# Linear attention into a channel mix on one core: halved crossbar transposes, g kept out of w_k for the first group, w_v loaded in two parts, and a new instruction order

## The chip, the cores and the metric

The kernel runs on one core of one Trainium2 chip. The metric is device time in microseconds (us): the time of one execution. Before the change it is 204.62 us, the median of 4 runs (204.26 to 205.23). The engines are named as in the profile: PE (TensorE, matrix multiply), PEld (its weight loads), DVE (VectorE), ACT (ScalarE), POOL (GpSimd) and SP (SyncE). Matrix operands are bf16 in on-chip memory; inputs and output are fp32 in device memory.

## The reference

Shapes are 8 batches, 8 heads, 576 positions, head width 64; the mix has model width 512 and hidden width 1024.

```python
def _attn_ref(q, k, v, g_norm):
    kv = np.einsum('bhsd,bhse->bhde', k, v)
    out = np.einsum('bhsd,bhde->bhse', q, kv)
    rms = np.sqrt(np.mean(out * out, axis=-1, keepdims=True) + 1e-06)
    return (out / rms * g_norm).astype(np.float32)

def _moe_ref(x, mu_k, mu_r, w_k, w_v, w_r):
    x_prev = np.concatenate([np.zeros((B, 1, D)), x[:, :-1, :]], axis=1)
    xk = mu_k * x + (1.0 - mu_k) * x_prev
    xr = mu_r * x + (1.0 - mu_r) * x_prev
    k = np.maximum(xk @ w_k, 0.0)
    v = k * k @ w_v
    r = 1.0 / (1.0 + np.exp(-(xr @ w_r)))
    return (r * v).astype(np.float32)
```

The attention output, with heads side by side, is the `x` of the second function. `g_norm` scales each head's 64 columns alike, so it may be multiplied into `x`, or into the rows of `w_k` and `w_r`.

## The kernel before

The work has two kinds of stage. Attention runs per batch (576 rows). The mix runs per group of 512 rows, so nine groups, numbered 0 to 8, cover the eight batches. Group 0 lies wholly in batch 0; group 1 needs the last 64 rows of batch 0 and most of batch 1, and so on.

The names below are those of the pieces in the order list; the number after the name is the batch or group, and what follows the point is a pair of heads (0 to 3), two of them for the larger batches, or a part. A `#2` marks the second use of a name; in batch 0 this is mostly the second stretch of columns.

Attention of a batch: `load` brings q, k and v by a GpSimd DMA that also converts to bf16. `kv` multiplies k by v on PE (`kvc` copies it out of PSUM). `qtr` transposes q on PE with `qc` copying it out, for batches 0 to 2. For batches 3 to 7 (`BY_DMA`) `ql` copies q into a buffer `q2` with pairs of heads side by side, `qt` transposes it with a DMA issued by SP, and `gate`, a one-element GpSimd copy that reads the transposed tile, holds the loads of the next batch until the transpose has landed: the loads follow `gate` in GpSimd's order. `u` multiplies q by kv on PE, `uc` copies it out, `sq` squares it, `ss` sums the squares on PE, `rr` is the reciprocal square root on ACT, and `mul` gives x, laid out so that the previous row is reached by an offset of 96 columns. For batches 5 to 7 the root goes through device memory (`ro`, `rb`). Then `d` is x minus the previous row; `mk`/`mr` scale it by mu, and `xk`/`xr` add the previous row.

Batch 0 is done in finer pieces, by one pair of heads for its first 256 rows and by two pairs for the other 320 (`mixed`, line 439), and the first half of group 0's k is summed pair by pair as the pairs arrive (`k0.a`, line 476); `k0.b` (line 763) is the rest.

The mix of a group: `k` (8 blocks of 128 hidden columns), `relu` on ACT, `ksq` on DVE, `r` and `sig` (line 795 and 800), `v` (line 817), `out` on DVE, which multiplies v by the sigmoid, and `store` by SP. The PSUM tiles of k, r and v come from one pool of two (`mm`); the output tiles from a pool of three, and `q2` has one buffer. A group's last step stands at line 834.

`w_k`, `w_r` and `w_v` are loaded by GpSimd. g is multiplied into `w_k` (two halves of hidden columns, `g.w_k0` and `g.w_k1`) and `w_r` in place on DVE, before any use.

All instructions stand in one list, `ORDER`: every piece in turn, with the engine after a colon where there is a choice. The list fixes the order within each engine's queue, SP's and GpSimd's DMA issues among them. `idle:n` puts n small matmuls on zeros into PE's queue. The costs, `land` and `due` values given to `add` were used to find an order and have no effect in the run.

```python
def load_w(dst, s, due, land, name):
    def fn(_):
        nc.gpsimd.dma_start(out=dst, in_=s.rearrange("(c p) n -> p c n", p=128))
...
gate = add({"POOL": 0.3}, lambda _: nc.gpsimd.tensor_copy(out=turned, in_=qT.t[0:1, 0, 0:1]), deps=[c],
```

Of the kernel before, what the change touches and what calls it, by code (L numbers as in the profile page):

```python
# [15 lines left out]
setup ident loadq0.2 loadk0.2 first_k first_q cast_q:DVE cast_k:DVE first_v table cast_v:DVE idle:61 qtr0.0  # L16
qc0.0#2:ACT idle:2 kv0.0 kvc0.0:ACT qtr0.1 qc0.1#2:ACT loadv0.2 idle:6 kv0.1 kvc0.1:ACT ident9 edge qc0.1:DVE
qc0.0:DVE idle:1 u0.0 uc0.0:DVE sq0.0 small tr9 u0.1 u0.0#2 uc0.1:ACT sq0.1 cols loadv0.6 loadk0.6 loadq0.4
uc0.0#2:ACT sq0.0#2 idle:5 ss0.0 rr0.0 mul0.0 idle:3 ss0.1 rr0.1 mul0.1 d0.0 mr0.0:DVE idle:1 ss0.0#2 rr0.0#2
mul0.0#2 kv0.3 kvc0.3:DVE d0.1 qtr0.2 qc0.2#2:ACT d0.0#2 mk0.0:DVE xk0.0 loadq0.6 qtr0.3 qc0.3#2:ACT qc0.3:ACT  # L20
loadv0.4 qc0.2:ACT loadk0.4 idle:7 kv0.2 idle:4 u0.3 uc0.3:DVE sq0.3 kvc0.2:ACT u0.2#2 uc0.2#2:ACT u0.2 uc0.2:ACT
sq0.2 idle:13 ss0.3 w_k0 g.w_k0 sq0.2#2 ss0.2 rr0.2 mul0.2 rr0.3 idle:8 ss0.2#2 rr0.2#2 d0.2 mul0.3 loadq1.0 k0.a0.0
idle:6 qtr1.0 mk0.0#2:ACT qc1.0:ACT mk0.2:DVE mul0.2#2 mr0.1#2:DVE loadk1.0 mk0.1#2:ACT mk0.1:DVE xr0.0 xk0.2
idle:14 k0.a0.2 loadv1.0 kv1.0 d0.2#2 xk0.1 k0.a0.1 mk0.2#2:DVE kvc1.0:ACT mr0.0#2:ACT u1.00 d0.3 mk0.3#2:DVE
mk0.3:DVE xk0.3 xk0.2#2 xk0.0#2 xr0.0#2 w_k1 uc1.00:ACT sq1.00 u1.01 uc1.01:ACT sq1.01 g.w_k1 mr0.2:DVE mr0.2#2:DVE
k0.a0.3 relu0.00 mr0.3:ACT k0.b0 ss1.00 k0.a1.0 relu0.10 mr0.1:DVE ksq0.10 xr0.2 ss1.01 rr1.01 rr1.00 k0.a1.3
k0.a1.1 k0.a1.2 relu0.01 mr0.3#2:ACT loadq1.4 w_r k0.b1 xr0.1 ksq0.00 xr0.3 loadv1.4 qtr1.2 loadk1.4 kv1.2 g.w_r:DVE
xr0.2#2 r0.2 relu0.11 qc1.2:DVE kvc1.2:DVE u1.10 uc1.10:ACT r0.3 sig0.1 u1.11 r0.0 r0.1 sig0.0 ksq0.11 ksq0.01
sq1.10 uc1.11:DVE sq1.11 ss1.11 ss1.10 rr1.10 mul1.0 d1.0 xk1.0 xr1.0 w_v v0.2.0 v0.2.1 v0.3.0 rr1.11 mul1.2 d1.2
xk1.2 v0.3.1 out0.1 v0.0.0 v0.0.1 v0.1.0 loadk2.0 loadq2.0 qtr2.2 qtr2.0 v0.1.1 qc2.0:DVE out0.0 qc2.2:ACT k1.0  # L30
loadv2.0 kv2.0 kvc2.0:ACT k1.1 relu1.0 xr1.2 loadq3.0 ql3.3:DVE ql3.0:DVE ql3.1:DVE ql3.2:ACT loadk3.0 loadv3.0
u2.10 uc2.10:DVE sq2.10 u2.01 uc2.01:ACT sq2.01 k1.2 k1.3 k1.4 u2.00 u2.11 store0.0#2 qt3 store0.0 store0.1#2
relu1.1 uc2.11:DVE uc2.00:ACT sq2.00 ksq1.1 sq2.11 ksq1.0 k1.5 ss2.01 rr2.01 relu1.2 k1.6 ss2.10 rr2.10 store0.1
gate3 loadq4.0 k1.7 relu1.3 ss2.00 rr2.00 mul2.0 r1.0 r1.1 sig1.0 r1.2 r1.3 ss2.11 sig1.1 loadv4.0 kv3.0 ksq1.2
ksq1.3 v1.0.0 v1.0.1 v1.1.0 v1.1.1 d2.0 xk2.0 rr2.11 kvc3.0:ACT u3.11 uc3.11:ACT u3.10 uc3.10:ACT v1.2.0 v1.2.1
u3.01 u3.00 uc3.01:ACT v1.3.0 v1.3.1 mul2.2 d2.2 out1.0 xk2.2 ql4.1:ACT uc3.00:ACT ql4.3:DVE loadk4.0 store1.0#2
store1.0 ql4.2:DVE ql4.0:DVE qt4 gate4 loadq5.0 out1.1 store1.1 k2.4 k2.5 relu2.2 sq3.00 sq3.10 xr2.2 sq3.01 sq3.11
ksq2.2 xr2.0 k2.6 k2.7 relu2.3 ksq2.3 k2.2 ss3.10 rr3.10 k2.3 relu2.1 ss3.11 rr3.11 mul3.2 ss3.00 k2.0 rr3.00 d3.2
k2.1 relu2.0 ss3.01 r2.0 rr3.01 mul3.0 ksq2.0 r2.1 sig2.0 kv4.0 r2.2 r2.3 kvc4.0:DVE ksq2.1 u4.10 u4.01 sig2.1
uc4.01:ACT uc4.10:ACT v2.0.0 v2.0.1 v2.1.0 xk3.2 d3.0 sq4.01 xk3.0 sq4.10 u4.11 uc4.11:ACT u4.00 ql5.2:DVE  # L40
uc4.00:ACT ql5.1:ACT sq4.11 ql5.3:DVE ql5.0:DVE loadk5.0 loadv5.0 v2.2.0 v2.2.1 v2.1.1 out2.0 ss4.10 rr4.10 v2.3.0
xr3.0 ss4.01 v2.3.1 out2.1 k3.4 k3.5 ss4.11 rr4.01 relu3.2 xr3.2 ksq3.2 k3.0 rr4.11 mul4.2 sq4.00 d4.2 xk4.2 k3.1
relu3.0 ksq3.0 qt5 store1.1#2 store2.1#2 k3.6 k3.7 kv5.0 kvc5.0:ACT relu3.3 k3.2 u5.10 uc5.10:DVE u5.11 uc5.11:ACT
ksq3.3 sq5.11 gate5 loadq6.0 k3.3 relu3.1 ksq3.1 u5.00 uc5.00:ACT sq5.00 u5.01 uc5.01:ACT r3.0 sq5.01 sq5.10 r3.1
sig3.0 ss4.00 ql6.3:ACT ql6.1:DVE ql6.2:DVE ql6.0:DVE store2.0#2 store2.0 store2.1 v3.0.0 v3.0.1 v3.1.0 v3.1.1
out3.0 rr4.00 mul4.0 d4.0 xk4.0 r3.2 ss5 r3.3 v3.2.0 v3.2.1 v3.3.0 v3.3.1 rr5 xr4.2 sig3.1 out3.1 xr4.0 loadv6.0
loadk6.0 kv6.0 k4.6 k4.7 relu4.3 k4.2 k4.3 kvc6.0:DVE qt6 u6.11 uc6.11:ACT ro5 relu4.1 store3.0 store3.0#2 u6.00
uc6.00:DVE sq6.00 k4.0 u6.01 uc6.01:ACT u6.10 uc6.10:DVE ksq4.3 k4.1 relu4.0 k4.4 k4.5 relu4.2 r4.0 r4.1 sig4.0
ksq4.1 ksq4.0 sq6.10 sq6.11 sq6.01 ss6 rr6 ro6 rb5 mul5.0 d5.0 gate6 loadq7.0 r4.2 ksq4.2 ql7.0:DVE ql7.3:DVE
ql7.2:DVE ql7.1:DVE xk5.0 mul5.2 r4.3 sig4.1 v4.2.0 v4.2.1 v4.3.0 v4.3.1 d5.2 xk5.2 out4.1 v4.0.0 v4.0.1 v4.1.0  # L50
v4.1.1 loadk7.0 loadv7.0 kv7.0 out4.0 xr5.2 k5.4 k5.5 relu5.2 k5.6 k5.7 kvc7.0:DVE xr5.0 qt7 u7.10 u7.01 uc7.10:DVE
# [51 lines left out]
def kernel(  # L103
# [97 lines left out]
    def dve_us(n, rate=1):  # L201
        return (0.13 if rate == 4 else 0.07) + n / rate / 960
# [696 lines left out]
```

## Time and profile before

| what | value |
|---|---|
| median of 4 runs | 204.62 us |
| the profiled execution: whole, and its span | 205.23 us, 203.4 us |
| PE busy | 194.3 us, 96% of the span, 1645 matmuls |
| DVE busy | 147.6 us, 73% |
| ACT busy | 113.6 us, 56% |
| POOL busy | 33.4 us, 16% |
| filler matmuls (line 713) | 131 |
| granted PE clock | full |
| mean DMA rate over the span | 156 GB/s |

The span is the time between the first and the last instruction of the profiled execution; the rest of its 205.23 us lies around it. Busy time of PE counts filler matmuls as well, and matmuls overlap, so it is no measure of useful work by itself. In the chain of waits each row is a start, a length and what the end of the kernel depended on there. In the timeline a row is a run of like instructions, with the engine's idle time before it and what ended it in brackets. In a table by windows each column after the stretch and its width is the busy time and count of one engine, then the granted clock, the DMA share and GB/s. A DMA row gives the number of issues, the KB of each and the microseconds from issue to landing.

### The profile page before, as it was taken

What the parts mean: (1) busy time and instruction counts of PE and PEld (TensorE: products, weight loads), DVE (VectorE), ACT (ScalarE), POOL (GpSimd) and SP (SyncE); (2) the same over time, 40 slices, a digit from 0 to 9 for tenths busy, and PEclk for the clock granted to TensorE, in tenths of its full rate; (3) what the DMA queues carried; (4) which work ended last, traced back from release to release, by engine and by line L of the source; (5) the groups of instructions that cost most, each with busy time, mean ns of one, the idle gap of its engine ahead of it and who ended that gap; (6) DMA issues with size and microseconds to landing.
All of it is one profiled execution on the core that took longest, in us unless ns stands there. A gap on an engine that the chain in (4) does not pass through costs nothing.

```text
span 203.4 us, 4096 instructions
## 1 busy us (share of the span) xinstructions
PE 194.3 (96%) x1645; PEld 102.6 (50%) x1645; DVE 147.6 (73%) x324; ACT 113.6 (56%) x145; POOL 33.4 (16%) x52
## 2 busy tenths in 40 slices
PE   7879699999999999999999999999999999999991
PEld 7757484454553454444447744444444444444451
DVE  1588968998589889799688799899658984232341
ACT  2276867827895598756992683286473226622500
POOL 6965404000050013005005202000200000000000
PEclk9999999999999999999999999999999999999999
DMA  6999999999989989998999999840180116000643
GB/s 177 195 202 205 204 205 206 204 203 219 197 174 182 226 162 124 202 206 188 215 199 221 180 196 159 232 140 3 52 220 3 42 37 205 29 0 0 179 131 108
DMA packets 39800, 31.69 MB, mean 156 GB/s; under 512 B 13636, under 2 KB 34916, under 8 KB 39780
## 3 DMA queue, kind: packets, MB, share of 16 engines
q0 software_dynamic: 21488, 18.11, 57.4%
q1 hardware_dynamic: 17620, 12.42, 25.8%
q10 hardware_dynamic: 672, 0.89, 1.3%
q8 instruction: 13, 0.21, 0.4%
q14 instruction: 7, 0.06, 0.1%
HBM read 35.33 MB, written 9.46 MB: 220 GB/s over the span
## 4 chain that ended last, share of the span: by engine, by line
PE 82%; DMA 8%; POOL 3%; ACT 2%; DVE 1%; issue 1%; SPq 0%; DVEq 0%
PE mm L743 26%; PE mm L817 24%; PE mm L795 15%; DMA qT<-q 5%; DMA k<-in_k_dram 4%; PE at L599 3%; PE at L520 3%; PE at L651 2%; PE mm L763 2%; PE at L834 2%; PE mm L834 2%; PE mm L476 2%; PE at L577 1%; ACT uT L184 1%; POOL q L273 1%
## 5 line engine op out<-in xcount | busy, mean ns | idle before, releaser
L743 PE MATMUL mm<-xk,w_k 128*128 128x512 bf16 (+1 forms) x288 | 59.0, 356 | 0.0
L817 PE MATMUL mm<-w_v,sqk 128*128 128x512 bf16 x256 | 58.3, 379 | 0.0
L747 ACT ACTIVATE relu<-mm 128x1024 bf16<-128x1024 f32 x36 | 37.0, 1027 | 36.2 <-PE mm L743 31.8
L743 PEld LDWEIGHTS <-w_k 128*128 128x128 bf16 x288 | 27.2, 98 | 26.1 <-issue 1.6
L817 PEld LDWEIGHTS <-sqk 128*128 128x128 bf16 x256 | 24.5, 98 | 29.1 <-issue 0.9
L795 PE MATMUL mm<-w_r,xr 128*128 128x512 bf16 x144 | 34.1, 380 | 0.0
L750 DVE TENSOR_TENSOR sqk<-relu 128x1024 bf16<-128x1024 bf16 x32 | 21.4, 686 | 12.0 <-ACT relu L747 11.8
L821 DVE TENSOR_TENSOR out<-mm,sig 128x1024 f32<-128x1024 f32 x16 | 19.5, 1221 | 12.8 <-PE mm L817 12.1
L800 ACT ACTIVATE sig<-mm 128x1024 bf16<-128x1024 f32 x18 | 18.3, 1024 | 16.7 <-PE mm L795 16.5
L795 PEld LDWEIGHTS <-xr 128*128 128x128 bf16 x144 | 13.4, 98 | 15.8 <-issue 0.9
L193 ACT ACT_TABLE_LOAD x14 | 18.0, 1283 | 1.4 <-PEq L883 1.2
L693 DVE TENSOR_SCALAR md<-d,cols 128x576 bf16<-128x576 bf16 x56 | 18.5, 371 | 0.3
L184 ACT CAST uT<-at 128x576 bf16<-128x576 f32 x21 | 12.8, 642 | 7.2 <-PE at L599 7.0
L667 DVE TENSOR_TENSOR xT<-uT,rs 128x1152 bf16<-128x1152 bf16 x14 | 10.5, 753 | 4.6 <-ACT rs L655 4.6
L713 PE MATMUL mm<-zero 128*128 128x128 bf16 x131 | 11.8, 253 | 1.1 <-DVE zero L243 1.1
L606 DVE TENSOR_TENSOR sq<-uT 128x576 bf16<-128x576 bf16 x28 | 11.9, 452 | 0.6 <-ACT uT L184 0.3
L655 ACT ACTIVATE rs<-at,eps 128x576 bf16<-128x576 f32 x16 | 11.6, 742 | 0.9 <-PE at L651 0.7
L634 POOL DMA_DIRECT2D rs<-rd x6 | 3.8, 642 | 45.6 <-DVE md L693 20.8
L713 PEld LDWEIGHTS <-zero 128*128 128x128 bf16 x131 | 10.0, 116 | 2.4 <-DVE zero L243 1.1
L696 DVE TENSOR_TENSOR xr<-md,xT 128x1152 bf16<-128x1152 bf16 x14 | 10.6, 759 | 0.5
L696 DVE TENSOR_TENSOR xk<-md,xT 128x1152 bf16<-128x1152 bf16 x14 | 10.6, 759 | 0.5
L679 DVE TENSOR_TENSOR d<-xT 128x1152 bf16<-128x1152 bf16 x14 | 10.6, 754 | 0.3
(81 smaller groups left out, 168.6 us busy)
## 6 DMA issues: line engine op xcount, KB each, us to landing
out_dram<-out SPq DMA_DIRECT2D x22, 192.0 KB, 2.5
k<-in_k_dram POOLq DMA_DIRECT2D x6, 576.0 KB, 13.4
q<-in_q_dram POOLq DMA_DIRECT2D x6, 576.0 KB, 8.5
v<-in_v_dram POOLq DMA_DIRECT2D x6, 576.0 KB, 12.0
out_dram<-out SPq DMA_DIRECT2D x23, 128.0 KB, 5.9
rs<-rd POOLq DMA_DIRECT2D x6, 288.0 KB, 5.7
out_dram<-out SPq DMA_DIRECT2D x22, 64.0 KB, 2.4
w_k<-in_moe_w_k_dram POOLq DMA_DIRECT2D x2, 512.0 KB, 10.6
```

The source lines that it names most:

```text
L184: nc.scalar.copy(out=dst, in_=src)
L193: nc.scalar.preload_act_table_set(name)
L693: nc.vector.tensor_scalar(out=get(md)[:, hp], in0=d.t[:, hp], scalar1=cols[:, m0 + hp:m0 + hp + 1], scalar2=None, op0=ALU.mult)
L696: nc.vector.tensor_tensor(out=dst[:, hs, c0:c0 + S], in0=md.t[:, hs], in1=xT.t[:, hs, 0:S], op=ALU.add)
L713: nc.tensor.matmul(get(k_ps[i])[:, 0, 0:128], zero[:, 0:128], zero[:, 128:256], start=not k_seen[i], stop=not k_seen[i])
L743: nc.tensor.matmul(get(ps)[:, fc % 2, a0:a1], w_k_sb[:, cc, 128 * fc:128 * fc + 128], xk[:, cc, x0:x0 + a1 - a0], start=(cc == 0), stop=(c ...
L747: nc.scalar.activation(out=get(rt), in_=ps.t, func=AF.Relu)
L750: nc.vector.tensor_mul(out=get(sqk)[:, 2 * f2:2 * f2 + 2, :], in0=rt.t, in1=rt.t)
L795: nc.tensor.matmul(get(ps)[:, ci % 2, :], xr[:, cc, n0:n0 + 128], w_r_sb[:, cc, :], start=(cc == 0), stop=(cc == NHP - 1))
L800: nc.scalar.activation(out=get(sg), in_=ps.t, func=AF.Sigmoid)
L817: nc.tensor.matmul(get(ps)[:, ci % 2, :], sqk.t[:, fc, 128 * ci:128 * ci + 128], w_v_sb[:, fc, :], start=(fc == 0), stop=(fc == NFC - 1))
L821: nc.vector.tensor_mul(out=get(ot)[:, xs, :], in0=ps.t[:, xs, :], in1=sg.t[:, xs, :])
```

## The change

It has four parts and an order that takes them up.

1. The DMA transpose of a batch (3 to 7) is issued as two, `qt.0` for the pairs of heads 0 and 1 and `qt.2` for 2 and 3; each waits for its own two relay copies, `u` waits for its half, and `gate` for the first half only.
2. For batch 0's rows in group 0 g goes into the k blend: `gcols` holds g·mu_k and g−g·mu_k. The blend is a scaling of the previous row (`gk`) and one fused multiply-add (`xk`), without the difference `d`; `d` and the r blend stay as they were. Group 0's k then reads `w_k` as loaded, and `w_k` is scaled by g in four quarters (`g.w_k00`, `g.w_k02`, `g.w_k10`, `g.w_k12`) after group 0's matmuls. The last 64 rows of batch 0, which belong to group 1, keep the former blend (`mt`, `xt`).
3. `w_v` is loaded in two halves, and each `v` piece waits for its own.
4. In the new order the first load of q stands ahead of `ident`; w_k and w_r are loaded behind q, k and v of the first half of batch 1; the load order within batches changes; stores of group 0's first output stand ahead of the first transpose; 137 fillers stand where 131 did.

```diff
 ORDER = """
-setup ident loadq0.2 loadk0.2 first_k first_q cast_q:DVE cast_k:DVE first_v table cast_v:DVE idle:61 qtr0.0
...
+setup loadq0.2 ident ident9 first_k first_q cast_q:DVE idle:61 qtr0.0 first_v cast_v:DVE cast_k:ACT idle:1 kv0.0
...
+xk0.0 d0.1 mr0.1:ACT xk0.1 mul0.3 xk0.1#2 mul0.2 mul0.2#2 gk0.2:DVE gk0.2#2:DVE d0.2#2 idle:11 qtr1.0 qc1.0:ACT
+gk0.3:DVE xk0.2 mr0.0:DVE xr0.0 kv1.0 kvc1.0:ACT idle:17 u1.01 u1.00 w_k0 idle:3 k0.a0.1 k0.a0.0 d0.2 xk0.3 k0.a0.2
+uc1.01:ACT gk0.3#2:ACT mr0.2:ACT sq1.01 ss1.01 k0.a0.3 rr1.01 relu0.00 xk0.3#2 xk0.2#2 w_k1 idle:6 k0.a1.3 k0.a1.2
...
+    def make_gcols(_):
+        nc.vector.tensor_scalar(out=gcols[:, 0:NHP], in0=cols[:, 0:NHP], scalar1=cols[:, 8:9], scalar2=None, op0=ALU.mult)
+        nc.vector.tensor_scalar(out=gcols[:, NHP:2 * NHP], in0=gcols[:, 0:NHP], scalar1=-1.0, scalar2=cols[:, 8:9],
+                                op0=ALU.mult, op1=ALU.add)
...
-    p_wv = load_w(w_v_sb, moe_w_v, -698, 5.2, "w_v")
+    p_wv = [load_w(w_v_sb[:, 4 * i:4 * i + 4, :], moe_w_v[C * i:C * i + C, :], -698 + 0.1 * i, 2.6, f"w_v{i}")
+            for i in range(2)]
...
+            def old(eng, hp):
+                by, w_ = gcols[:, NHP + hp:NHP + hp + 1], slice(c0, min(c1, G))
...
+            def fused(_, hp):
+                w_ = slice(c0, min(c1, G))
+                nc.vector.scalar_tensor_tensor(out=xk[:, hp, w_], in0=xT.t[:, hp, NP + c0:NP + min(c1, G)],
+                                               scalar=gcols[:, hp:hp + 1], in1=mds["k"].t[:, hp, w_],
+                                               op0=ALU.mult, op1=ALU.add)
...
-            c = add({"SP": 3.1}, q_turn, deps=parts, bufs=[q2, qT], land=3.4, name=f"qt{b}", **when("qc", 0))
-            qtc = {hp: c for hp in range(NHP)}
+            qtc = {}
+            for hp in (0, 2):
+                c = add({"SP": 1.6}, lambda _, hs=slice(hp, hp + 2): q_turn(_, hs), deps=parts[hp:hp + 2], bufs=[q2, qT],
+                        land=1.7, name=f"qt{b}.{hp}", **when("qc", 0))
+                qtc[hp] = qtc[hp + 1] = c
             if b + 1 < B:
-                gate = add({"POOL": 0.3}, lambda _: nc.gpsimd.tensor_copy(out=turned, in_=qT.t[0:1, 0, 0:1]), deps=[c],
-                           bufs=[qT], name=f"gate{b}")
+                gate = add({"POOL": 0.3}, lambda _: nc.gpsimd.tensor_copy(out=turned, in_=qT.t[0:1, 0, 0:1]),
+                           deps=[qtc[0]], bufs=[qT], name=f"gate{b}")
...
+            for i in range(2):
+                cs = slice(512 * i, 512 * i + 512)
+                p_wk[i] = [scale_w(w_k_sb[:, c2:c2 + 2, cs], p_wk[i][0], None, f"g.w_k{i}{c2}",
+                                   {"DVE": dve_us(1024, 4), "ACT": act_us(1024, True, True)}, wk_users[i])
+                           for c2 in (0, 2)]
```

## The prediction

> **What bounds the kernel now.** I read the page first, then the chain of waits in order of time, the timeline of PE and of DVE, the windows of the first 31 us, and the DMA issues one by one.
>
> ```profile
> PE 194.3 (96%) x1645; PEld 102.6 (50%) x1645; DVE 147.6 (73%) x324; ACT 113.6 (56%) x145; POOL 33.4 (16%) x52
> PE   7879699999999999999999999999999999999991
> DMA  6999999999989989998999999840180116000643
> ```
>
> TensorE is at 9 tenths from the seventh slice to the last. In the PE timeline the only wait after 31 us is 0.16 us, in the single row below.
>
> ```profile
> 29.17 1.75 PE mm L763 x16
> 30.92 0.63 PE at L577 x24
> 31.55 0.38 PE at L520 x24
> 31.93 0.97 PE mm L795 x4
> ...
> 197.51 1.76 PE at L834 x16
> 199.30 0.42 DVE out L841
> ```
> ```profile
> 132.14 0.44 PE L599 MATMUL at<-qT,kv 64*64 64x288 bf16 x8 [0.16 <-DMA qT<-q]
> ```
>
> In the chain, k of group 0 ends at 30.92, and from there to 199.30 it is nearly all matmuls. Neither the 131 filler matmuls nor the gaps ahead of that point are work. So the change can gain only by reaching the state "k of group 0 done" earlier, and lose only by opening a hole later. What limits the opening:
>
> ```profile
> 18.00:20.00 2.00, 1.84 (x40) 1.51 (x38) 1.87 (x10) 1.70 (x4) 1.11 (x2) 1.00 1.28 209
> 20.00:22.00 2.00, 1.98 (x45) 1.58 (x44) 2.00 (x10) 1.58 (x2) 1.31 (x2) 1.00 1.26 202
> 22.00:24.00 2.00, 1.48 (x18) 0.81 (x17) 1.97 (x7) 1.86 (x5) 0.24 (x1) 1.00 1.28 206
> 24.00:26.00 2.00, 0.97 (x9) 0.87 (x9) 2.00 (x7) 1.37 (x3) 0.77 (x1) 1.00 1.26 204
> ```
> ```profile
> 7.43 7.40 DMA k<-in_k_dram
> 14.87 0.38 PE a L361 x12
> ```
>
> After the width come PE, weight loads, then DVE, ACT, POOL: DVE is busy 7.84 of 8 us, while PE, fillers included, has holes. DMA runs flat at some 200 GB/s. Batch 0's last load (k, heads 4 and 5) lands at 14.83; from there the chain is kv, u, square, rms, multiply and blend on DVE.
>
> **What the Trainium skill says.** "VectorE: DVE Perf Modes", section "The perf-mode tier table", has bf16 tensor_scalar at four elements a cycle and tensor_tensor at two; scalar_tensor_tensor has no row. The trace agrees for large tiles: two scalings of 576 take 0.65 us, one subtraction of 1152 takes 0.76; at 256 elements both step by 0.20 from start to start (DVE timeline below), so the fixed part decides.
>
> ```profile
> 19.35 0.28 DVE L451 TENSOR_SCALAR md<-d,cols 128x256 bf16<-128x256 bf16 x1
> 19.55 0.52 DVE L422 TENSOR_TENSOR xT<-uT,rs 128x384 bf16<-128x384 bf16 x2
> 19.99 0.49 DVE L451 TENSOR_SCALAR md<-d,cols 128x320 bf16<-128x320 bf16 x2
> 20.39 0.28 DVE L455 TENSOR_TENSOR xr<-md,xT 128x256 bf16<-128x256 bf16 x1
> 20.60 0.28 DVE L455 TENSOR_TENSOR xk<-md,xT 128x256 bf16<-128x256 bf16 x1
> 20.80 0.48 DVE L443 TENSOR_TENSOR d<-xT 128x640 bf16<-128x640 bf16 x1
> ```
>
> "DMA: Bandwidth & Descriptors", section "SWDGE vs HWDGE vs iDMA", says that each engine takes turns between the queues fed by GpSimd and by SP, so stores and transposes slow the loads in flight. The trace shows it: loads of 576 KB land 2.9 us apart from 41.5 to 50.2, and the next, beside a transpose, 3.9 later. The same page, "Latency and other measured facts", gives a DMA transpose 261 GB/s; here 576 KB take 6.7 us from issue, 88 GB/s, and the measurement decides.
>
> **The change part by part.** Times are those of the profiled execution (span 203.4, 205.23 whole); it lies 0.6 above the median 204.62, so I take the difference from the median.
>
> *Loads.* Per-load issues and times to landing in the DMA view (below, w_k's first and second) give a serial queue: w_k's first half lands at 16.8, then q, k, v of batch 1 to 21.2, second half 23.6, q 25.2, w_r 27.7, v, k 30.65, w_v 35.7. After, w_k0 goes behind q, k, v of batch 1: the same set of bytes, so w_k0 lands near 21.2, w_k1 23.6, w_r 23.6+2.5=26.1, w_v's halves at 33.2 and 35.7. The first load no longer waits for `ident` (1.6 us of POOL waiting). DMA idles for the first 1.8 us, so I take 0.5 off everything (bounds 0 and 0.75, the move of the second issue): k of heads 4 and 5 at 14.3, w_k1 at 23.1. The two w_v loads cost one more issue of 0.8 on a POOL that idles.
>
> ```profile
> w_k<-in_moe_w_k_dram POOLq DMA_DIRECT2D x1, 512.0 KB, 8.7
> w_k<-in_moe_w_k_dram POOLq DMA_DIRECT2D x1, 512.0 KB, 12.5
> ```
>
> *g moved from w_k.* Two scalings (0.75 and 0.85) leave the front of DVE's queue. They return as four of half that size, about 0.35 each, three on DVE, one on ACT, after group 0 has read the raw w_k; plus 0.3 for two [128,4] operations, and four 64-wide scalings and two adds, 0.1 to 0.15 each. The first of the four, g.w_k02, makes DVE wait for k0.b0's end near 29.7; queued behind it are ksq0.10, the copies of qtr1.2 and kv1.2 and sq1.11, sq1.10, which by the same steps end at 35.5, while PE asks for their ss at 35.65: just covered. The k blend no longer needs the difference: scale by g(1-mu) (0.20), then one scalar_tensor_tensor. Its price isn't in the trace: not below the 0.20 of a 256-wide add, and at one element a cycle, as the 384-wide copy from PSUM (0.56) suggests, 0.56-128/960=0.43. I take 0.36; eight of them.
>
> *The walk to r of group 0.* From k at 14.3, ACT copies kv, q and u one after another (0.42+0.21+0.49+0.48) and DVE starts sq0.3 at 16.0 (16.49 before). In its new order, by start-to-start steps of before: squares and a PSUM copy 0.28+0.56+0.28+0.36=1.48; four gk up to gk0.3, 0.81; five fused blends up to xk0.3, 1.80; d 0.20+0.40+0.20; three multiplies 0.40+0.40+0.44; mr and xr 0.40. Together 6.53, so xk0.3 at 22.5, and sq1.01 at 22.95. PE has ss1.01 queued in front of k0.a0.3, so that starts at 23.25 with w_k0 long there; 0.44 for it, 0.4 for six fillers, 1.75 for k0.a1, 0.24 for ss1.00, 1.83+1.75 for k0.b1 and k0.b0: 29.7. DVE meanwhile, from 22.95: two blends 0.72, PSUM copy 0.65, d, sq, mr 0.80, a blend 0.36, two scalings of 320 0.46, a square 0.61, xr 0.40, w_r 0.77, and mr, mt and xr pieces 1.43: all xr at 29.15, just ahead of PE. So r starts at 29.7 where the same set of work stood at 30.92: **1.2 earlier**.
>
> *Holds after that.* w_v: r, qtr, kv, r, u, r need 5.1 us, so v0.0.0 comes at 34.8 (first half 32.7) and v0.2.1 at 37 (second 35.2): hidden; undivided, the load at 35.2 would have cost 0.4. ACT must finish sig0.0 by 36.1 to free PSUM, behind two uT copies: on the edge, I charge 0.1. Batch 2: kv2 would start at 45.1 (r to kv2 is 15.4 us of PE's durations); its last load lands near 43.9, plus up to 1.2 because all four stores of out0.0 (512 KB, 2.6 us at 200 GB/s, shared with the loads) now issue near 42: cover of about 1.3, just enough.
>
> *Transposes.* One issue of SP takes 3.4 to 5.9 us, landing 6.7 to 6.8 (9.8 once). A half isn't shown: landing 3.4 if all scales, 4.4 if only the issue part does; above that if there is a larger fixed part. I take 4.4, and the second 6.8 after the first's issue. Since the gate opens at the first half, each turn load-relay-transpose shortens by 2.3 (19 us now, 56.1 to 75.3). The turn isn't on PE's path now (waits of POOL for it, 51.6 us, cost nothing), so it pays nothing in itself; it pays for PE needing qT 3 to 5 us sooner in the new order. By PE's work end to end, u6 comes at 107.5 and u7 at 128 (112.19 and 132.14 before). The relay of q6 stands on DVE after out2.1, which PE lets start at 84.7, with two outs (2.3), two xr (2.6), a multiply (0.95), a difference (0.67), an xk (1.3), five squares of u (1.85) and four of k (2.44): 96.8, with small waits 97.3, and 1.8 for the copies, 99.1. Both halves land at 105.9: 1.6 to spare. SP queues behind a waiting half the stores of groups 1 to 3; three output buffers and two more groups of time cover them.
>
> *New order.* PE issues the same real matmuls (1513 beside 137 instead of 131 fillers), and changes between small and full tiles as often. The altered land costs in `load` steer nothing at run time.
>
> Sum: -1.2+0.1 = -1.1, from 204.6 to **203.5**.
>
> **The rivals.**
> - *Planned in full, 202.5.* If DVE's fused blends cost 0.25 and xk0.3 is ready by 22, the second half of w_k at 23.1 is the only limit: r at 23.1+1.75+0.24+3.58=28.7, 2.2 earlier, 0.1 given back. For it: w_k1 was waited for before, too. Against: DVE is full.
> - *Nothing left, 204.5.* k of heads 4 and 5 still lands at 14.8 (+0.5), the fused blends cost 0.46 (+0.5 over five). Or the stores push batch 2's last load 1 us past kv2. For it: that load landed 2.4 after its neighbour, which an earlier first issue may not cure.
> - *Slower, 206.1.* Halves carry a fixed part, and the loads released at the first half slow the second. For it: the last transpose, with loads in flight, took 9.8. Place: u6, whose first piece in PE's order uses the second half. The pair, issued at 99.1, may take 8.4 us; beyond that PE stands still. At 5.5 a half it is 11, a hole of 2.6: -1.1+2.6. Against: batch 6's loads, issued from about 87, should have landed by then.
> - That the change doesn't do what it says: the instruction order shows ten half transposes and gates on the first, so I give it nothing.
>
> **How the numbers follow.** About 0.3% (0.6 us) is what a measurement can tell. Forecast 0.36 (202.9 to 204.0), full 0.19, nothing left 0.19, slower 0.26. Faster: 0.32+0.19+0.03=0.54; same: 0.04+0.15+0.02=0.21; slower 0.25. The range runs from 202.0, past the full plan, to 206.0, which leaves out half the slow case. Faster cases alone: 202.0 to 204.1.
>
> **What would show it.** Right: r of group 0 starting near 29.7, fused blends near 0.36 on a full DVE, k0.a0.3 waiting for ss1.01, no PE gap at kv2 or u6. Wrong: PE waiting for DMA qT or k after 40; DVE busy and r after 30.5; a first half landing more than 5.5 after its issue.

## The result, and the profile after

| | before | after |
|---|---|---|
| median | 204.58 us (64 runs, 203.94 to 207.03) | 203.93 us (43 runs, 202.77 to 206.51) |
| ratio to before | | 0.9959, 95% interval 0.9947 to 0.9971 |
| the profiled execution: whole, span | 205.23, 203.4 | 203.81, 202.0 |
| group 0's k done, next piece starts | 30.85 | 28.57 |
| last matmul ends | 199.26 | 197.97 |

The change makes the kernel 0.4% faster: 0.65 us between the medians, 0.8 by the ratio. The last two rows are read from PE's timelines, the end as start plus length of the last row. Ratios are of undisturbed runs alone; of the kernel with whole transposes three runs of six, the profiled one among them, were slower at a lower granted clock, so its time is the median of the other three and the waits of its profile are read for their place and not for their size.

The page of the kernel after: busy times, and the span in 40 slices.

```profile
PE 194.3 (96%) x1651; PEld 103.2 (51%) x1651; DVE 147.7 (73%) x332; ACT 116.1 (57%) x148; POOL 32.8 (16%) x53
...
PE   7999999999999999999997999999999999999991
...
DMA  6999999999969999999999948830742240003273
```

The shares are those of before. New is a 7 in PE's row between the 9s, a little past the middle of the span. The windows of the same kernel show the other side: in the stretches from 20 to 26 us, where PE had holes before (1.98, 1.48 and 0.97 busy of 2.00), it now works almost without one, and DVE is as full as it was.

```profile
20.00:22.00 2.00, 1.96 (x23) 1.36 (x16) 1.97 (x8) 1.55 (x3) 0.79 (x1) 1.00 1.25 208
22.00:24.00 2.00, 1.93 (x21) 1.74 (x21) 2.00 (x7) 1.48 (x2) 0.59 (x1) 1.00 1.24 205
24.00:26.00 2.00, 2.00 (x21) 1.77 (x19) 2.00 (x8) 1.14 (x2) 0.24 (x2) 1.00 1.30 202
```

PE's timeline of the kernel after, at the places that the prediction spoke of: the first part of group 0's k (line 522), its second part (815), r (853), kv of batch 2 (567), and the end of the stretch before u of batch 6 (649).

```profile
20.47 1.48 PE L522 MATMUL mm<-xk,w_k 128*128 128x256 bf16 x12
22.07 0.40 PE L701 MATMUL at<-sq,ones 128*128 128x288 bf16 x2
22.32 0.60 PE L522 MATMUL mm<-xk,w_k 128*128 128x256 bf16 x4
...
25.08 3.66 PE L815 MATMUL mm<-xk,w_k 128*128 128x256 bf16 x32
28.57 1.89 PE L853 MATMUL mm<-w_r,xr 128*128 128x512 bf16 x8
...
44.08 0.95 PE L567 MATMUL at<-v,k 96*64 96x64 bf16 x48
...
106.51 1.04 PE L795 MATMUL mm<-xk,w_k 128*128 128x256 bf16 x8
108.62 0.44 PE L649 MATMUL at<-qT,kv 64*64 64x288 bf16 x8 [1.08 <-DMA qT<-q]
...
196.06 1.91 PE L892 MATMUL at<-w_v,sqk 128*128 128x256 bf16 x16
```

Group 0's r starts at 28.57, and no bracket stands at kv of batch 2. At u6, the multiplication of batch 6's q by kv, PE waits 1.08 us for a half transpose. Besides it only 0.15 at 56.84 (for a sigmoid) is left after 28.57. The chain of waits of the same kernel says which half:

```profile
98.65 1.93 SPq L603
100.58 0.04 issue
100.62 7.96 DMA qT<-q
108.58 0.04 issue
108.62 0.44 PE at L649 x8
```

The first half of T6, the transpose of batch 6's q, is issued at 98.65 and the second at 100.62. The chain follows the second: it lands at 108.58, 7.96 after its own issue and 9.93 after the first's. The first half had landed by 104.50, when the gate behind it opened:

```profile
104.50 0.22 POOL L612 COPY turned<-qT 1x1 bf16<-1x1 bf16 x1 [1.46 <-DMA qT<-q]
```

So the opening won about two microseconds against the profile of before, and u6 gave one back.

### The profile page after: what moved, and what is told of

Read it like the earlier page. It is cut to its first block, busy times and chain, and to the rows that moved or that the text cites. A ratio compares the mean times of both kernels' runs of the same rounds, so it can differ in the third digit from the quotient of the medians.

```text
span 202.0 us, 4138 instructions
## 1 busy us (share of the span) xinstructions
PE 194.3 (96%) x1651; PEld 103.2 (51%) x1651; DVE 147.7 (73%) x332; ACT 116.1 (57%) x148; POOL 32.8 (16%) x53
## 4 chain that ended last, share of the span: by engine, by line
PE 78%; DMA 10%; DVE 4%; ACT 3%; SPq 2%; issue 1%; DVEq 0%; POOLq 0%; ACTq 0%
PE mm L795 28%; PE mm L875 24%; PE mm L853 13%; DMA qT<-q 4%; DMA k<-in_k_dram 3%; DMA q<-in_q_dram 3%; PE at L649 2%; PE at L567 2%; PE mm L815 2%; PE at L892 2%; PE mm L892 2%; PE at L701 2%; PE mm L522 1%; DVE xk L478 1%; SPq L603 1%
## 5 line engine op out<-in xcount | busy, mean ns | idle before, releaser
L853 PE MATMUL mm<-w_r,xr 128*128 128x512 bf16 x144 | 34.6, 380 | 0.0
L879 DVE TENSOR_TENSOR out<-mm,sig 128x1024 f32<-128x1024 f32 x16 | 19.5, 1222 | 19.4 <-PE mm L875 15.7
L802 DVE TENSOR_TENSOR sqk<-relu 128x1024 bf16<-128x1024 bf16 x32 | 21.7, 686 | 10.6 <-ACT relu L799 10.4
L763 PE MATMUL mm<-zero 128*128 128x128 bf16 x137 | 12.3, 250 | 1.1 <-DVE zero L245 1.1
L763 PEld LDWEIGHTS <-zero 128*128 128x128 bf16 x137 | 10.4, 115 | 2.6 <-DVE zero L245 1.1
## 6 DMA issues: line engine op xcount, KB each, us to landing
q<-in_q_dram POOLq DMA_DIRECT2D x6, 576.0 KB, 10.4
```

The costliest lines, as they stand in the source:

```text
L763: nc.tensor.matmul(get(k_ps[i])[:, 0, 0:128], zero[:, 0:128], zero[:, 128:256], start=not k_seen[i], stop=not k_seen[i])
L802: nc.vector.tensor_mul(out=get(sqk)[:, 2 * f2:2 * f2 + 2, :], in0=rt.t, in1=rt.t)
L853: nc.tensor.matmul(get(ps)[:, ci % 2, :], xr[:, cc, n0:n0 + 128], w_r_sb[:, cc, :], start=(cc == 0), stop=(cc == NHP - 1))
L879: nc.vector.tensor_mul(out=get(ot)[:, xs, :], in0=ps.t[:, xs, :], in1=sg.t[:, xs, :])
```

## The experiments

Twelve runs follow, two of them of unaltered kernels. "r" is the start of the piece that follows group 0's k on PE. The ratio is to the kernel before, measured on the same chip; the interval is 95%. kv7 is the multiplication of k by v of batch 7, v0 the first piece of group 0's v.

| what is altered | r | waits of PE later on | span | ratio |
|---|---|---|---|---|
| nothing (kernel before) | 30.05 | none above 0.2 | 202.4 | not taken |
| nothing (kernel after) | 28.54 | u6 1.10 | 202.1 | 0.9966 [0.9949, 0.9983] |
| first load of q behind `ident` | 28.66 | kv7 0.23 | 201.3 | 0.997 [0.9955, 0.9985] |
| 4 more additions on DVE | 29.29 | none above 0.2 | 202.1 | 0.9993 [0.9971, 1.0014] |
| opening: three moves | 28.61 | kv7 0.22 | 201.3 | 0.995 [0.993, 0.997] |
| g scaled into w_k ahead | 29.62 | kv7 0.78 | 202.4 | 0.9975 [0.9962, 0.9988] |
| w_v in one load | 28.59 | v0 1.06 | 202.3 | 1.0014 [0.9993, 1.0034] |
| whole transposes | | u6 and three more | | 1.0362 [1.0334, 1.039] |
| k4 ahead of u6 | 28.54 | sums of squares of batch 6, 0.36 | 201.9 | 0.9973 [0.9958, 0.9989] |
| u6: first half first | 28.57 | none above 0.2 | 200.9 | 0.9946 [0.9929, 0.9964] |
| that and the opening | 28.38 | kv7 0.17 | 201.0 | 0.9943 [0.9929, 0.9957] |
| that and T6 sooner | 28.70 | kv7 1.09 | 202.2 | 0.9959 [0.9933, 0.9984] |

### The kernel before, again

No edit: a second profiled execution of the kernel before.

> The kernel before once more, for a second profile. Theory A (the profiled execution of before was an unlucky one: it lies 0.6 us above its own median, and its load of k for heads 4 and 5 landed 2.4 us after its neighbour): here that load lands near 14.2 instead of 14.83, r of group 0 starts near 31.2 instead of 31.9, and the span is near 202.8. Theory B (that load is late in every execution, and the spread comes from elsewhere): it lands at 14.8 again and r starts at 31.9 again.

Measured: 204.13 us whole, span 202.4. PE's timeline (line 361 is kv of heads 4 and 5, 763 is k0.b, 577 and 520 are the transposes and kv that follow it):

```profile
13.72 0.38 PE L361 MATMUL a<-v,k 96*64 96x64 bf16 x12
...
28.21 1.91 PE L763 MATMUL mm<-xk,w_k 128*128 128x256 bf16 x16
30.05 0.70 PE L577 MATMUL at<-ident,q 96*64 96x96 bf16 x24
30.58 0.54 PE L520 MATMUL at<-v,k 96*64 96x64 bf16 x24
31.06 1.04 PE L795 MATMUL mm<-w_r,xr 128*128 128x512 bf16 x4
```

Here group 0's k ends at 30.05, not 30.85, and r starts at 31.06: theory A, and more than it said. In the first profile PE waited 1.24 us for the last k load of batch 0, until 14.87; here the matmuls that need it start at 13.72 without a wait. So the profile on which the prediction rests had a late opening: 0.8 of the 2.3 by which the change seems to lead was scatter of one landing. Against this execution the opening gains 30.05-28.57=1.5.

### The kernel after, again

> The changed kernel unaltered, a second profiled execution beside the runs below. Theory A, the opening repeats and the wait at u6 doesn't: r of group 0 again at 28.5 to 28.7, set by the landing of w_k's first half (20.4 to 21.0) and the work of TensorE behind it, while the landing of the second half of T6 scatters by up to 1 us, so the wait at L649 is anything between 0 and 1.1; ratio 0.995 to 0.998. Theory B, the wait is systematic: 0.9 to 1.2 again at u6.

Measured: 203.64 us median, r at 28.54. In PE's timeline of this second execution the wait at u6 is there again:

```profile
108.61 0.44 PE L649 MATMUL at<-qT,kv 64*64 64x288 bf16 x8 [1.10 <-DMA qT<-q]
```

The opening repeats to 0.03 and the wait to 0.02 (theory B). Both profiled executions of this kernel have the wait; two profiles of other kernels with the same order at u6 don't, as the section on the swap shows. Both ends can now be set against each other. From group 0's k to PE's end it is 198.24-30.05=168.2 us in the kernel before and 197.97-28.54=169.4 after; the difference is the 1.10 at u6 and the 0.15 at 56.8.

### The first load of q behind `ident` again

```diff
-setup loadq0.2 ident ident9 first_k
+setup ident loadq0.2 ident9 first_k
```

> The changed kernel with the first load of q behind the making of ident again. Theory A (the opening is a chain from the landing of batch 0's last load of k, 13.62 us in the changed kernel, through a full DVE to r of group 0): that load lands 0.4 to 0.8 later, r of group 0 starts as much later, and the time rises by 0.3 to 0.8 us. Theory B (DVE or the load of w_k binds on its own): r starts within 0.15 us of 28.6 and the time stays.

Measured: 203.87 us, ratio 0.997, r at 28.66, 0.1 later than in the kernel after. Lines of PE's timeline (371 is kv of heads 4 and 5):

```profile
12.83 0.38 PE L371 MATMUL a<-v,k 96*64 96x64 bf16 x12
...
20.84 1.48 PE L522 MATMUL mm<-xk,w_k 128*128 128x256 bf16 x12 [0.73 <-DMA w_k<-in_moe_w_k_dram]
...
28.66 1.67 PE L853 MATMUL mm<-w_r,xr 128*128 128x512 bf16 x7
```

The k load that theory A expected later was in use at 12.83, earlier than in the kernel after (13.66), and r didn't follow it: theory B. PE waits here for the first half of w_k, and DVE isn't late. In the two profiles of the kernel after, the chain of waits ahead of 22 us goes through the k load (landing 13.62 and 13.58) and then along DVE; here, and in the swapped kernel below, it goes through the w_k load, issued at 10.02 and in use at 20.84. The two limits lie within 0.4 us of each other, and moving the first load ahead of `ident` is worth nothing that shows. The k load scatters more than this move could give: it was in use at 12.8 to 14.2 in the profiles of the new order.

### Four more additions on DVE ahead of xk0.3

```diff
+    def pad(_):
+        for _i in range(4):
+            nc.vector.tensor_tensor(out=scr, in0=zero, in1=zero, op=ALU.add)
...
-k0.a0.1 k0.a0.0 d0.2 xk0.3 k0.a0.2
+k0.a0.1 k0.a0.0 d0.2 pad xk0.3 k0.a0.2
```

> Four more 256-wide bf16 additions on DVE (0.20 each from start to start, 0.8 in all) right ahead of the blend xk0.3; their output is not used. Theory A, DVE has become less than full ahead of r: the chain from w_k's landing through PE sets r, and 0.8 more on DVE moves r by less than 0.4 (ratio to before up to 0.998). Theory B, DVE is the limit beside it, as the prediction had it: every 0.1 on DVE moves r by 0.1, k0.a0.3 starts at 23.1 instead of 22.3 and r at 29.3 to 29.4, ratio about 0.9995.

Measured: r at 29.29, ratio 0.9993. On DVE the four took 1.18 from their own start (20.72) to that of the blend xk0.3 behind them (21.90). PE's timeline:

```profile
20.77 1.48 PE L529 MATMUL mm<-xk,w_k 128*128 128x256 bf16 x12 [0.73 <-DMA w_k<-in_moe_w_k_dram]
22.79 0.41 PE L708 MATMUL at<-sq,ones 128*128 128x288 bf16 x2 [0.54 <-DVE sq L663]
...
29.29 1.89 PE L860 MATMUL mm<-w_r,xr 128*128 128x512 bf16 x8
```

DVE's timeline at xk0.3, first the kernel after, then this one:

```profile
21.18 0.48 DVE L478 SCALAR_TENSOR_TENSOR xk<-xT,gcols,md 128x256 bf16<-128x256 bf16 x1
```
```profile
21.90 0.47 DVE L485 SCALAR_TENSOR_TENSOR xk<-xT,gcols,md 128x256 bf16<-128x256 bf16 x1
```

PE first waits for w_k, then for DVE's square, and r moves by 29.29-28.57=0.72 for 1.18 of extra work. DVE was 20.97-20.51=0.46 earlier ahead of the additions in this execution, so the blend itself starts 21.90-21.18=0.72 later, and r moves by just that. This is theory B: DVE still sets r, beside the load of w_k.

### Three moves in the opening

```diff
-sq1.01 ss1.01 k0.a0.3 rr1.01 relu0.00 xk0.3#2 xk0.2#2 w_k1 idle:6 k0.a1.3
+sq1.01 k0.a0.3 ss1.01 relu0.00 rr1.01 xk0.3#2 xk0.2#2 w_k1 k0.a1.3
...
-xr0.1 mr0.0#2:DVE mt0.3:DVE xr0.3 xr0.0#2 mt0.2:DVE xr0.2
+xr0.1 mr0.0#2:DVE xr0.3 xr0.0#2 xr0.2 mt0.3:DVE mt0.2:DVE
```

> Three moves in the opening: the sum of squares ss1.01 goes behind k0.a0.3, the six fillers before k0.a1.3 go, and the two 64-wide scalings for group 1 go behind the last xr piece. Theory A, with w_k's first half landed at 20.4 what is left is PE's own queue and the last pieces of DVE: k0.a0.3 starts at 22.0 instead of 22.3, k0.a1 at about 22.7 instead of 23.09, k0.b at 24.7 to 24.8 (the second blend of heads 0 and 1 is ready at 24.63), r of group 0 at about 28.2 instead of 28.57, ratio about 0.9945. Theory B, DVE binds from here on and PE waits where the fillers were: r at 28.5 or later, ratio 0.996 as without the moves.

Measured: 203.15 us, ratio 0.995, r at 28.61. PE started k0.a0 only at 21.04 in this execution, 0.57 later than in the kernel after, and still r came at the same time: from k0.a0 to r it is 7.57 us, in the kernel after 28.57-20.47=8.10. So the moves take 0.5 off PE's own path. The first half of w_k landed at 20.95 here (9.85+11.1), at 20.39 in the kernel after (9.99+10.4), so its landing decides whether that is worth anything. The ratio doesn't tell it from none, and the wait at u6, which stood in both profiles of the kernel after, is absent from this one. The run decides nothing by itself.

### g back in w_k, inside the new order

```diff
+        p_wk.append([scale_w(w_k_sb[:, :, cs], l, None, f"g.w_k{i}", {"DVE": both["DVE"]})])
...
-gk0.3:DVE xk0.2
+d0.3 mk0.3:DVE xk0.2
...
-idle:3 k0.a0.1 k0.a0.0 d0.2 xk0.3
+idle:3 g.w_k0:DVE k0.a0.1 k0.a0.0 xk0.3
...
-w_k1 idle:6 k0.a1.3
+w_k1 idle:6 g.w_k1:DVE k0.a1.3
```

> The part with g is undone inside the new order: batch 0 has the former blend again (difference, scaling by mu, add; the differences of heads 2 to 7 stand ahead of their scalings), and w_k is scaled by g in two halves on DVE before group 0 reads it, the first half ahead of k0.a0.1, the second ahead of k0.a1.3. Loads and all else stay in the new order. Theory A, a good part of the opening gain is that the scaling of w_k left the path: PE now waits for the landing at 20.4 plus 0.75 before it starts k0.a0, for a scaling of 0.75 to 0.85 more before k0.a1 (landed 22.0), and DVE has that much more ahead of the second blends; r of group 0 at 29.2 to 29.8, ratio 0.999 to 1.002. Theory B, the new order of the loads and pieces alone brings the gain, and DVE has the room for the two scalings: r at 28.9 or earlier, ratio below 0.998.

Measured: 203.77 us, ratio 0.9975, r at 29.62. PE's timeline:

```profile
21.80 1.48 PE L478 MATMUL mm<-xk,w_k 128*128 128x256 bf16 x12 [0.94 <-DVE w_k L313]
...
29.62 1.89 PE L804 MATMUL mm<-w_r,xr 128*128 128x512 bf16 x8
...
117.34 0.95 PE L523 MATMUL at<-v,k 96*64 96x64 bf16 x48 [0.78 <-DMA v<-in_v_dram]
```

PE waits for the scaling, and r comes 1.05 later, as theory A had it. This part alone carries some 1.05 of the 1.5 that the opening gains; the k load was in use 0.2 later in this execution (13.86), which may account for as much of it. But the ratio rises by only 0.0009 against the second run of the kernel after (on another chip), within both intervals, where 1.05 us would be 0.005: in the time the part isn't shown. The last line shows part of the reason: this execution has no wait at u6 (it asks 0.7 later), but one of 0.78 at kv of batch 7, for that batch's load of v.

### w_v in one load

```diff
-    p_wv = [load_w(w_v_sb[:, 4 * i:4 * i + 4, :], moe_w_v[C * i:C * i + C, :], -698 + 0.1 * i, 2.6, f"w_v{i}")
-            for i in range(2)]
+    p_wv = [load_w(w_v_sb, moe_w_v, -698, 5.2, "w_v")] * 2
```

> w_v is loaded in one piece of 1024 KB again, issued where its first half stood; every v piece waits for all of it. Theory A, the split is needed: in the changed kernel the halves land at 32.4 and 35.0 and TensorE asks for w_v at 33.6, so v0.0.0 waits until 35.0, a hole of 1.4 at 33.6, and nothing later gives it back: ratio 1.001 to 1.003. Theory B, a single load lands earlier than the two (one fixed part less) and the later waits for DMA take up what is lost: hole below 0.8, ratio below 0.999. The prediction on record put the cost of an undivided load at 0.4.

Measured: 204.55 us, ratio 1.0014. PE's timeline at the first v piece:

```profile
34.85 1.04 PE L874 MATMUL mm<-w_v,sqk 128*128 128x512 bf16 x4 [1.06 <-DMA w_v<-in_moe_w_v_dram]
```

In the kernel after this piece starts at 33.62 without a wait; its halves land at 32.4 and 35.0 (issue plus time to landing, 16.24+16.2 and 17.72+17.3), the whole at 34.8. The hole is 1.06, between the theories' bounds, and the ratio is A's: against the kernel after on the same chip (0.9966) it loses 0.0048, or 1.0 us, and the intervals don't meet. Without the split nothing of the gain is left.

### Whole transposes in the new order

```diff
-            for hp in (0, 2):
-                c = add({"SP": 1.6}, lambda _, hs=slice(hp, hp + 2): q_turn(_, hs), deps=parts[hp:hp + 2], bufs=[q2, qT],
...
+            c = add({"SP": 3.1}, q_turn, deps=parts, bufs=[q2, qT], land=3.4, name=f"qt{b}", **when("qc", 0))
...
-                           deps=[qtc[0]], bufs=[qT], name=f"gate{b}")
+                gate = add({"POOL": 0.3}, lambda _: nc.gpsimd.tensor_copy(out=turned, in_=qT.t[0:1, 0, 0:1]), deps=[c],
```

> The changed kernel with one transpose for all four pairs of heads again, the gate behind it, everything else as changed; the whole stands where the first half stood (for batch 7 where its last relay copy is done). Theory A (a half takes 5 to 6.7 us to land, as long as the whole took before, and the second comes 2 to 3 us after it, so the split gives nothing): gates open within 1 us of the changed kernel's, PE's wait at u6 shrinks from 1.08 to 0.5 or less, the time is equal or up to 0.7 us lower. Theory B (as predicted: the first half is needed, since each turn of load, relay and transpose becomes 2.3 us shorter by it): the gates drift later by about 2 us a turn, u6 and u7 wait 2 to 6 us, the time rises by more than 1.5 us.

Measured: 211.98 us, ratio 1.0362. The waits in PE's timeline, for their places only:

```profile
87.03 0.41 PE L698 MATMUL at<-sq,ones 128*128 128x288 bf16 x2 [2.08 <-DVE md L740]
108.15 0.95 PE L567 MATMUL at<-v,k 96*64 96x64 bf16 x48 [0.81 <-DMA v<-in_v_dram]
116.47 0.70 PE L646 MATMUL at<-qT,kv 64*64 64x288 bf16 x8 [5.54 <-DMA qT<-q]
140.19 0.44 PE L646 MATMUL at<-qT,kv 64*64 64x288 bf16 x8 [2.05 <-DMA qT<-q]
```

The new order without the halves is 3.6% slower than before. That is theory B. The halved transposes are not an extra: the order asks for qT at 107.5, four to five microseconds ahead of the order before (111.39 and 112.19), and without the halves load, relay and transpose don't follow. The run doesn't separate the smaller transfers from the gate that opens at the first of them.

### k of group 4 ahead of u6

```diff
-out3.1 k4.4 qt6.0 qt6.2 store3.0#2 store2.0#2 u6.10 u6.01 uc6.01:ACT k4.5 relu4.2
+out3.1 k4.4 k4.5 relu4.2 k4.2 qt6.0 qt6.2 store3.0#2 store2.0#2 u6.10 u6.01 uc6.01:ACT
```

> The changed kernel with two blocks of k of group 4 (k4.5 and k4.2, 1.7 us of PE) moved ahead of u6.10, so that PE asks for the second half of batch 6's transpose near 109.3 instead of 107.5. Theory A (the 1.08 us wait of PE for that half is a loss on the path that nothing gives back): the wait is gone and the time falls by 0.9 to 1.1 us against the changed kernel, ratio to before near 0.991. Theory B (PE only idles there instead of a little later, since the data of batch 6 and the sigmoid of group 4 come when they come): the time stays within 0.3 us of the changed kernel, ratio near 0.996.

Measured: 203.83 us, ratio 0.9973. PE's timeline:

```profile
109.19 0.44 PE L649 MATMUL at<-qT,kv 64*64 64x288 bf16 x8
...
115.79 1.04 PE L671 MATMUL at<-sq,sel 128*32 128x288 bf16 x8 [0.36 <-DVE sq L656]
```

u6 doesn't wait, but the sums of squares of batch 6 (line 671) do: their row takes 1.04 where the kernel after needs 0.43, after a wait of 0.36, together 0.97. Putting work ahead of u6 delays DVE's copies and squares of it. The hole has moved, as theory B had it: the ratio is no better than that of the kernel after (0.9959 and 0.9966).

### u6: the half that lands first is used first

```diff
-u6.10 u6.01 uc6.01:ACT k4.5 relu4.2 uc6.10:DVE sq6.10
+u6.00 u6.01 uc6.01:ACT k4.5 relu4.2 uc6.00:DVE sq6.00
...
-u6.00 ksq4.2 uc6.00:ACT sq6.00 u6.11
+u6.10 ksq4.2 uc6.10:ACT sq6.10 u6.11
```

> The two pieces of u of batch 6 that read the first half of the transpose (u6.00, u6.01) stand ahead of the two that read the second half (u6.10, u6.11); nothing else moves, the copies and squares take the places of those they are swapped with. Theory A, the order of the two halves at u6 is what costs: the changed kernel's first piece of u6 is u6.10, which needs the second half at 108.6, while the first half is there by 104.5; swapped, PE goes through at 107.5 and asks for the second half only at about 111.7. No wait at L649 near 108, none at the sums of squares of batch 6 either, the span about 1 us shorter than 202.0, ratio to before about 0.991 (0.9959 without the swap). Theory B, the wait only moves: DVE, which copies and squares u6 at the same time as it finishes batch 5, is behind as well, and a wait of 0.5 to 1 appears near 115 at L671, ratio 0.995 to 0.997. Theory C, the hole of 1.08 is that of one execution and in the median one it is near 0.2: no wait, but the ratio changes by less than 0.002.

Measured: 203.3 us, ratio 0.9946. PE's timeline:

```profile
107.47 0.44 PE L649 MATMUL at<-qT,kv 64*64 64x288 bf16 x8
107.84 2.79 PE L795 MATMUL mm<-xk,w_k 128*128 128x256 bf16 x24
110.56 0.44 PE L649 MATMUL at<-qT,kv 64*64 64x288 bf16 x8
...
194.92 1.91 PE L892 MATMUL at<-w_v,sqk 128*128 128x256 bf16 x16
```

No wait at u6, none above 0.1 behind it, and PE's last matmul ends at 196.83, 1.14 ahead of the kernel after, with r at the same 28.57. That is A's trace. But the swap isn't shown to be its reason. Two profiles of kernels with the old order at u6 (`ident` and the opening moves) have no wait there either; this line is of the first:

```profile
107.55 0.44 PE L649 MATMUL at<-qT,kv 64*64 64x288 bf16 x8
```

So with the old order the second half lands before 107.5 in some executions, and this may be one like them. By ratio the swap is 0.3 to 0.4 us faster than the kernel after (0.9946 beside 0.9959 and 0.9966), between A and C, and the intervals overlap. What speaks for the swap is the demand: PE now asks for the second half at 110.56 only, and in no profile of an order with halves in which its landing can be read (108.3 to 108.8) did it land later than that.

### The swap and the opening moves together

The edits of the last experiment and of the opening moves.

> The swap at u6 and the three moves of the opening together. Theory A, the two act in different places and add up: r of group 0 at w_k's landing plus 7.6 (28.1 to 28.6), no wait at u6, ratio 0.992 to 0.994. Theory B, what is gained ahead is waited for at kv of batch 7, whose v lands about 10.5 after an issue that hangs on the gate of batch 6 (104.5 in the changed kernel): a wait of 0.2 to 0.8 at L567 near 116, ratio 0.9945 to 0.996.

Measured: 203.14 us, ratio 0.9943, the lowest of all. PE's timeline:

```profile
20.48 1.92 PE L522 MATMUL mm<-xk,w_k 128*128 128x256 bf16 x16 [0.22 <-DMA w_k<-in_moe_w_k_dram]
...
22.89 1.92 PE L522 MATMUL mm<-xk,w_k 128*128 128x256 bf16 x16 [0.24 <-DMA w_k<-in_moe_w_k_dram]
...
28.38 1.89 PE L853 MATMUL mm<-w_r,xr 128*128 128x512 bf16 x7
...
115.79 0.95 PE L567 MATMUL at<-v,k 96*64 96x64 bf16 x48 [0.17 <-DMA v<-in_v_dram]
```

In this execution PE waits for both halves of w_k, so the loads alone bind the opening; and at 115.79 it waits 0.17 for v of batch 7, just under what B had. The ratio is hardly below that of either edit alone (0.9946 and 0.995), which speaks for B, but the intervals are too wide to exclude that they add up. Beside the kernel after on the same chip (0.9966) the gain is 0.0023, and the two intervals overlap; in the trace PE ends at 196.87 instead of 197.97.

### The first half of T6 ahead of two stores

```diff
-ro5 store2.1 r3.1
+ro5 qt6.0 store2.1 r3.1
...
-k4.4 qt6.0 qt6.2 store3.0#2
+k4.4 qt6.2 store3.0#2
```

On top of the kernel above.

> As the kernel with the swap at u6 and the three opening moves, and the first half of T6 is issued ahead of the two stores of out2.1 (1.2 us of SP) that stood between the load rd and it. Theory A, the turn of batch 6 binds at kv7: T6's first half is issued near 98.0 instead of 98.65, gate 6 opens at 103.0 to 103.5, v of batch 7 lands before 115.3, and no wait is left at u6 or kv7; ratio 0.991 to 0.993. Theory B, the turn is late for another reason (the relay copies of q6 end at 97.9, or the halves slow one another): gate 6 at 103.6 or later, and no difference beyond 0.001 from the kernel without the move.

Measured: 203.37 us, ratio 0.9959. GpSimd's timeline, first the kernel without the move, then with it (`rs<-rd` brings the reciprocal roots of batch 5 back, `turned<-qT` is the gate):

```profile
101.45 1.26 POOL L684 DMA_DIRECT2D rs<-rd  x2 [11.45 <-DMA rd<-rc]
103.83 0.55 POOL L612 COPY turned<-qT 1x1 bf16<-1x1 bf16 x1 [1.12 <-DMA qT<-q]
```
```profile
103.37 1.27 POOL L684 DMA_DIRECT2D rs<-rd  x2 [12.67 <-DMA rd<-rc]
104.62 0.35 POOL L612 COPY turned<-qT 1x1 bf16<-1x1 bf16 x1
```

The half was issued at 98.20 instead of 98.45, yet the gate opened 0.8 later, without a bracket: the half had landed. What held the gate stands ahead of it in GpSimd's queue, the issue of `rs<-rd`, which waits for the write `rd`. From the issue of that write to the load it took 103.37-96.78=6.6 us instead of 101.45-96.46=5.0. v of batch 7 then came late, with a wait of 1.09 at kv7. B was right that nothing is gained; its reasons weren't those found. In the ten profiles of other kernels with halves, where the first half was issued 2.0 us behind the write, the same stretch is 4.6 to 5.1 us. That the transpose close behind slows the small write is likely; a second profile of this order wasn't taken.

## Why the prediction was right or wrong

**The bound: right.** From group 0's k to the end PE needs 168.2 to 168.3 us in the kernel before (second profile) and in the swapped one (196.83-28.57). All differences are the start of that stretch and holes in it. The forecast itself, 203.5 beside 203.93 measured, lies inside its range; the sum behind it is another matter.

**The landing of k of heads 4 and 5: mis-sized, and for a wrong reason.** It was put at 14.3, 0.5 ahead of the profile, credited to the load that no longer waits for `ident`. It was 13.62, and in the kernel before, seen again, the work behind it started at 13.72. The row of 14.83 was scatter. The move of `ident` is worth nothing that shows. Nor does r follow this load alone: with the same opening it was in use at 12.94, 12.99 and 12.83 (k4 ahead of u6, the swap, `ident`), 0.7 to 0.8 earlier, and r came at 28.54 to 28.66 all the same, behind the load of w_k.

**The walk to xk0.3: right in sum.** From sq0.3 to the end of xk0.3 the forecast had 22.5-16.0=6.5; the chain of waits has 15.09 to 21.65, 6.56. The five blends took 1.98 there instead of 1.80, the squares with the copy and the multiplies 0.25 less together. DVE's timeline shows the price of a fused blend in its first pair of starts:

```profile
16.57 0.48 DVE L478 SCALAR_TENSOR_TENSOR xk<-xT,gcols,md 128x256 bf16<-128x256 bf16 x1
16.96 0.28 DVE L453 TENSOR_TENSOR d<-xT 128x256 bf16<-128x256 bf16 x1
```

0.39 from start to start where 0.36 was taken: within the bounds, near the upper one. (The upper bound's 960 elements a microsecond is also what the trace gives: copies from PSUM of 576 and 384 elements take 0.76 and 0.56, 192 elements in 0.20.) What was off is only the start of the walk, 15.09 instead of 16.0, with the load.

**r of group 0: 28.57 instead of 29.7.** In the profiled execution all but 0.2 of this is that start. "1.2 earlier" was thus wrong twice, by the start after and by that before: against a like execution the gain is 1.5. The rival "planned in full" named r at 28.7 and a limit by the load of w_k; the place was right, though it is the first half (in use at 20.5 to 21.0) as much as the second that binds. The forecast saw w_k's first half "long there" by 23.25; it is one of two limits 0.4 us apart.

**g out of w_k: right in sign.** It is worth some 1.05 at r, though nothing that shows in the time. The quarters returned without being felt: PE starts v0.0.0 at 33.62 with no wait, 34.8 having been forecast.

**w_v: hidden, as said; the cover was thinner.** Undivided it costs 1.06 on PE, not 0.4, because PE is there earlier. The 0.1 charged for the first sigmoid didn't come: no wait stands in PE's timeline between 28.57 and 56.84.

**Batch 2's loads: right.** kv2 starts at 44.08 (45.1 forecast) without a wait, the stores ahead of them notwithstanding. The last load landed at 43.74 (25.94+17.8), so the cover was 0.3 and not 1.3: PE came earlier, the load didn't.

**The halves of the transpose: the step that failed.** "I take 4.4, and the second 6.8 after the first's issue ... Both halves land at 105.9: 1.6 to spare." SP's and GpSimd's timelines give from a first half's issue to its gate 6.7, 5.1, 6.7 and 5.9 us (49.34 to 56.05, 66.66 to 71.78, 80.41 to 87.12, 98.65 to 104.50), for 288 KB; the five whole ones of the kernel before, 576 KB, took 6.7 to 9.8. A half takes nearly as long as a whole. The second half of T6 landed 9.93 after the first's issue. The Trainium skill's 261 GB/s for a DMA transpose ("DMA: Bandwidth & Descriptors", section "Latency and other measured facts") isn't met here: 288 KB in 5.1 us from issue to landing is 58 GB/s. With 9.9 the forecast's own issue at 99.1 would have given 109.0 against PE's 107.5, a hole of 1.5; with the measured issue, 98.65, it is 108.6, the hole that came. Two of the prediction's own signs of being wrong came with it: PE waiting for qT after 40, and first halves landing more than 5.5 after their issue.

What else stands in that step was partly right and partly lucky. u6 was asked for at 107.5 as computed, but from r to u6 PE needed 107.47-28.57=78.9 where the forecast's figures leave 107.5-29.7=77.8; r came earlier by as much. The relay of q6, forecast to end at 99.1, was done at 97.9. The turns of load, relay and transpose became shorter, by 1.3 us each on average and not by 2.3 (gate to gate 15.7, 15.3 and 17.4 after; 19.2, 16.3 and 16.9 before, the last to T6's landing). The rival "slower" had the place, u6 and its second half, and a price of 11 for the pair; its sign was wrong because the pair took 9.9 and the opening gained more than it allowed. Its mechanism is open. Against it the prediction set that batch 6's loads should have landed by then; they hadn't. v of batch 6 landed at 103.5 (89.90+13.6), 4.9 us after T6's first issue.

**The sum.** Between the second profile of before and that of after: -1.5 in the opening, +1.2 in holes, -0.3 at PE's end; against the first profile of before -2.3 and +1.1, net of the hole of 0.16 that went away, where PE's ends differ by -1.29. The medians lie between, at -0.65. The forecast of -1.1 came near because two errors offset each other in part: the opening was taken too small, and the hole not at all. That is luck. What makes the second half take 7.96 from its own issue, a fixed part in each half, the four stores issued on SP right behind it, the loads that the gate lets go, or the batch's own loads still in flight, wasn't tried. On the last the traces have a hint: v of batch 6 landed at 103.5 and 103.25 in the two executions with the hole, at 102.4 and 101.6 in the two with the old order at u6 and second halves there by 107.5. Four profiles that agree are no test.

## What to carry to other kernels

Before sizing a gain in the opening, compare at least two executions: here the landing at the head of the chain was 1.1 us later in one profile than in the next. When a transfer is split, work out the last piece's landing and let the consumer use the first piece first; here the order had it the other way round at u6, and PE stood still for 1.1 us in two profiles. With an engine that is solid to the end, look for the chain of transfers that stands closest behind it, since that is where an earlier start is waited away.

## What the runs showed of the hardware

- A DMA transpose of 288 KB took 5.1 to 6.7 us from issue to gate (four first halves), one of 576 KB 6.7 to 9.8 (five), with loads in flight in every case: the time follows the bytes only weakly here. Two halves issued 2.0 us apart needed 9.9 and 10.0 us in two executions and at most 8.8 in three others.
- A scalar_tensor_tensor of 128x256 in bf16 steps by 0.39 us on DVE, as long as a 256-wide scaling and a 256-wide add together (0.20 each).
- Between the issue of a small write and the load that waits for it lay 6.6 us when a transpose was issued 1.4 us behind the write (one profile), 4.6 to 5.1 when it came 2.0 us behind (ten profiles).
